# A gated linear attention kernel: one tile per column block of w_in, and the second group's alpha ahead of the first scores

## The chip, the cores and the metric

The kernel runs on one core of a Trainium2 chip. The metric is the device time of one execution in microseconds (us); the time before is the median of three runs. The engines are named as the profile names them: PE is the matrix engine (PEld its weight loads), DVE the vector engine, ACT the scalar engine, POOL the general one, SP the engine that issues most transfers. A name with a q at its end (SPq) is an engine's sequencer.

## The reference

Two blocks follow each other. The first is a gated linear attention with 4 batches, 8 heads, 768 steps and 48 values per head; the second projects its output with `w_in`, runs a decaying sum over time, gates it and projects it with `w_out`. Both weights come as float64.

```python
for t in range(S):                                   # attention, per batch and head
    state = alpha[t, :, None] * state + outer(k[t], v[t])
    y[t] = q[t] @ state
x = y.transpose(0, 2, 1, 3).reshape(B, S, H * D)     # 4 x 768 x 384
proj = x @ w_in                                      # w_in 384 x 1024, float64
val, gate = proj[..., :512], proj[..., 512:]
for t in range(S):
    h = exp(A_log)[0] * h + val[:, t, :]
    ys[:, t, :] = h
out = (gate * sigmoid(gate) * ys) @ w_out            # w_out 512 x 384, float64
```

## The kernel before, in words

The 4 x 768 steps are cut into 12 groups of 256 steps, two chunks (c = 0, 1) of 128 steps each. All instructions stand in an order that is written out by hand, engine by engine in program order; an engine that waits holds up everything behind it on that engine. The steps of one group m:

- Loading: SP issues the transfers of alpha, k, q (`load_natural` for groups 0 to 2, `load_raw` later) and v. The weights follow group 1 on SP's queue: for each of four column blocks i of 128 columns of the value half and of the gate half, `load_w_in(i)` issues eight transfers into `bits_in`, 32 in all; then two transfers bring `w_out` into `bits_out`, and group 2's inputs come behind those.
- `natural_alpha(m)`: PE turns alpha by 8 transposes, ACT copies it into `aT`. `check_alpha(m)`: one ACT instruction (with a read of its sum) that looks whether alpha stays at or below one.
- `products(m)`, a generator: DVE forms the running product `prod` over the group (a scan, L606), then its inverse `inv` (a scan, L618).
- `natural_qk(m, name)`: PE turns k or q, DVE multiplies with `inv` or `prod` into `Z` (L580). In the kernel before, these PSUM tiles come from the pool of the scores' banks.
- `scores(m, c)`: 16 matmuls of k against q into `sc0` and `sc1`. `masks(m, c)`: the triangular mask, on DVE for `sc0` (L660), on ACT (a copy, L658) and POOL (L659) for `sc1`. `keys(m, c)`: PE turns k back, ACT copies it to `ktm` (L643). `state`, `values`, `carried`: matmuls for the running state and the output y. `join(m)`: ACT copies y into `xT`, and six small transfers move its fourth quarter into place (L707); for groups 0 and 1 POOL issues them.
- `project(n, cc)`: six accumulating products of xT with block cc of `w_in`, the value half (pv) and the gate half (pg). `gated(n, cc)`: a DVE scan over pv (hh, L730), ACT's Silu of pg (sg, L735), POOL's product f (L736). `output(n)`: 16 matmuls with `w_out` (the first 12 need the first three blocks of f, the last four the fourth block).

The weights must be made float32 once. `convert(i)` does so for block i of `w_in` (i = 0 to 3) or for a half of `w_out` (i = 4, 5): ACT makes a low part `wr` (L517), DVE forms the high part with a TENSOR_SCALAR (L518) and a SCALAR_TENSOR_TENSOR (L520), and POOL adds the two (L522). The call gives back the addition, so that it can be placed apart: `convert(0)()` or `sums = convert(3)` and later `sums()`. The same instruction order has, before the loop, group 0's and group 1's attention, with the six conversions and `project(0, 0)` to `project(0, 3)` between and behind them; then `output(0)`; then the loop over n = 1 to 11, which mixes the projection of group n with the attention of group n + 1.

`w_in` and `bits_in` are one tile each; a conversion reads a quarter of `bits_in` and writes a quarter of `w_in`, each quarter in strips. The waits between engines and on transfers are set by the program from the tiles that instructions read and write.

`check_w(i)` scans the raw weights' size on DVE (two reductions each), in the loop from n = 3 on. `warm(count)` issues matmuls that nothing reads.

Of the kernel before, what the change touches and what calls it, by code (L numbers as in the profile page):

```python
# [346 lines left out]
def fast(  # L347
# [86 lines left out]

    w_in = const.tile([C, NK, 2, DI], FP32, name="w_in")
    w_out = const.tile([C, NI, DM], FP32, name="w_out")
    NW = NK + 2
    bits_in = const.tile([C, NK, 2 * DI, 2], U32, name="bits_in")
    bits_out = const.tile([C, NI, DM, 2], U32, name="bits_out")

    def load_w_in(i, engine):

        for first_row, size in ((0, D), (D, R)):
            for vg in range(2):
                for s in range(2):
                    row, step = (4 * s * D, D) if size == D else ((4 * s + 3) * D, R)
                    cols = ds(2 * (vg * DI + i * C), 2 * C)
                    engine.dma_start(  # L448
                        out=bits_in[ds(64 * s + first_row, size), :, ds(vg * DI + i * C, C)]
                        .rearrange("p kk n two -> p kk (n two)"),  # L450
                        in_=moe_w_in.bitcast(U32)[ds(row, NK * step), cols]
                        .rearrange("(kk p) n -> p kk n", p=step)[0:size])
# [51 lines left out]
    def convert(i):  # L504


        if i < NI:
            bits = bits_in.rearrange("p kk (vg n) two -> p kk vg n two", vg=2)[:, :, :, ds(i * C, C)]
            w = w_in[:, :, :, ds(i * C, C)]
        else:  # L510
            rows = ds(2 * (i - NI), 2)
            bits, w = bits_out[:, rows, None], w_out[:, rows, None, :]
# [11 lines left out]
    def check_w(i):  # L524
        if i < NK:
            hi = bits_in[:, i, :, 1].bitcast(FP32)
        else:
            hi = bits_out[:, ds(2 * (i - NK), 2)].rearrange("p cc n two -> p (cc n) two")[:, :, 1].bitcast(FP32)
        for t, op in ((wmax, ALU.max), (wmin, ALU.min)):
# [35 lines left out]

    def natural_qk(m, name):

# [3 lines left out]
        for c in range(G):  # L571
            tp = ps_sc.tile([C, 4, C], FP32, tag=f"sc{c}", name="tn")
            for p in range(4):
# [140 lines left out]
    def project(n, cc):  # L714
# [6 lines left out]
        for vg, pj in enumerate((pv, pg)):  # L721
            for kk in range(NK):
                nc.tensor.matmul(pj, w_in[:, kk, vg, ds(cc * C, C)], xT[:, kk, :],  # L723
                                 start=(kk == 0), stop=(kk == NK - 1))
# [73 lines left out]
    for _ in products(0):  # L798
        pass
    for c in range(G):  # L800
        k_times(c)
        q_times(c)
    for c in range(G):
        scores(0, c)
# [3 lines left out]
    for c in range(G):  # L808
        keys(0, c)
    natural_alpha(1)  # L810
    check_alpha(1)
    steps = products(1)
    next(steps)
    next(steps)
    values(0, 0)
# [4 lines left out]
    join(0, (nc.gpsimd, nc.gpsimd))()  # L820
    k_times, q_times = natural_qk(1, "k"), natural_qk(1, "q")
    warm(4)
    for _ in steps:
        pass
    for c in range(G):
        k_times(c)
        q_times(c)
    convert(0)()

# [4 lines left out]
    for c in range(G):  # L834
        keys(1, c)
    convert(1)()
    pj = project(0, 0)
    gated(0, 0, *pj)
    state(1, 0)
# [4 lines left out]
    carried(1, 1)  # L844
    convert(2)()
    join(1, (nc.gpsimd, nc.gpsimd))()
    sums = convert(3)
    pj = project(0, 1)
    gated(0, 1, *pj)
    sums()  # L850
    sums = convert(NI)
    pj = project(0, 2)
    gated(0, 2, *pj)
    sums()
    natural_alpha(2)
    sums = convert(NI + 1)
    pj = project(0, 3)
    gated(0, 3, *pj)
    sums()
    check_alpha(2)  # L860
# [103 lines left out]
```

## Time and profile before

| what | value |
|---|---|
| median of three runs | 327.07 us (324.81 to 328.57) |
| profiled execution | 329.01 us |
| its span, first to last instruction | 327.3 us |
| PE busy | 296.7 us (91%) |
| DVE, ACT, POOL busy | 230.7, 96.9, 115.1 us |
| mean granted clock of PE | 0.961 of full |
| transfers | 39.71 MB, mean 121 GB/s |

A row of the timeline gives the start in the span, the time, the engine, the line of the code, the operation, what is written and read, and how many instructions are merged; in brackets the idle time of that engine before it and what ended it. The granted clock is 1.00 where PE runs at its full level (2.4 GHz) and 0.50 at the lower one (1.2 GHz).

### The profile page before, as it was taken

The numbers are of one execution on the slowest core, as the hardware profiler recorded it, in microseconds if no ns is written. First come the engines' busy times: TensorE is split into PE (matmuls) and PEld (weight loads), VectorE is DVE, ScalarE is ACT, GpSimd is POOL, SyncE is SP. The second block draws the span as 40 slices with busy tenths as digits, with TensorE's granted clock in tenths as the row PEclk, the third lists the DMA queues.
The fourth block names the chain that finished last, engine by engine and source line by source line (L and its number), as shares of the span: only waits on it lengthen the run. The fifth ranks groups of instructions, "written<-read, shape, count | busy, mean of one in ns | idle before, by whom it ended". The sixth has DMA issues, their size and how long they took to land.

```text
span 327.3 us, 6026 instructions
## 1 busy us (share of the span) xinstructions
PE 296.7 (91%) x2355; PEld 232.4 (71%) x2355; DVE 230.7 (70%) x244; ACT 96.9 (30%) x201; POOL 115.1 (35%) x109
## 2 busy tenths in 40 slices
PE   8898089579996999999999999999999999999991
PEld 4485078348865887878868878878688688786870
DVE  3864297958972696898997998989979689432110
ACT  3270226304120433324224224242253143221201
POOL 6032096821800521721704306408133054140120
PEclk9999669959996999999999999999999999999999
DMA  9998899708159904936909819759169220100101
GB/s 135 163 182 194 234 215 218 122 0 203 33 117 214 196 8 119 216 60 170 204 16 246 130 58 225 112 141 215 35 177 199 62 50 11 52 1 14 48 5 55
DMA packets 69165, 39.71 MB, mean 121 GB/s; under 512 B 47492, under 2 KB 68616, under 8 KB 69128
## 3 DMA queue, kind: packets, MB, share of 16 engines
q1 hardware_dynamic: 66736, 38.35, 59.2%
q10 hardware_dynamic: 2008, 0.69, 1.0%
q8 instruction: 20, 0.33, 0.5%
q0 software_dynamic: 384, 0.20, 0.3%
q14 instruction: 17, 0.14, 0.1%
HBM read 33.33 MB, written 4.72 MB: 116 GB/s over the span
## 4 chain that ended last, share of the span: by engine, by line
PE 80%; SPq 7%; DMA 4%; DVE 3%; POOL 2%; issue 1%; ACT 0%; POOLq 0%
PE pv L723 21%; PE o L744 20%; PE pg L723 18%; PE sc L652 6%; PE y L671 6%; DMA bits_in<-in_moe_w_in_dram 4%; SPq L421 4%; PE y L682 3%; PE st L692 3%; SPq L448 2%; PE tp L642 2%; DVE w_out L520 2%; SPq L430 1%; POOL w_out L522 1%; DVE hh L730 1%
## 5 line engine op out<-in xcount | busy, mean ns | idle before, releaser
L736 POOL TENSOR_TENSOR f<-sg,hh 128x256 f32<-128x256 f32 x48 | 60.3, 1257 | 151.8 <-ACT sg L735 135.0
L723 PE MATMUL pv<-xT,w_in 128*128 128x256 f32 x288 | 75.3, 399 | 16.0 <-POOL w_in L522 12.6
L723 PEld LDWEIGHTS pv<-xT,w_in 128*128 128x128 f32 x288 | 54.2, 195 | 29.2 <-POOL w_in L522 13.5
L723 PE MATMUL pg<-xT,w_in 128*128 128x256 f32 x288 | 71.8, 386 | 0.0
L744 PE MATMUL o<-w_out,f 128*128 128x384 f32 x192 | 67.1, 504 | 4.3 <-POOL w_out L522 4.3
L723 PEld LDWEIGHTS pg<-xT,w_in 128*128 128x128 f32 x288 | 56.1, 195 | 8.1
L744 PEld LDWEIGHTS o<-w_out,f 128*128 128x128 f32 x192 | 37.7, 197 | 29.0 <-POOL w_out L522 4.9
L735 ACT ACTIVATE sg<-pg 128x256 f32<-128x256 f32 x48 | 18.4, 383 | 111.6 <-PE pg L723 92.7
L730 DVE TENSOR_TENSOR_SCAN hh<-a_dec,hh,pv 128x256 f32<-128x256 f32 x32 | 23.5, 734 | 38.5 <-PE pv L723 36.6
L659 POOL TENSOR_TENSOR A<-A,mask 128x512 f32<-128x512 f32 x24 | 31.0, 1312 | 28.0 <-ACT A L658 28.0
L606 DVE TENSOR_TENSOR_SCAN prod<-aT,first 128x1024 f32<-128x1024 f32 x12 | 32.9, 2746 | 0.1
L618 DVE TENSOR_TENSOR_SCAN inv<-aT,last 128x1025 f32<-128x1025 f32 x12 | 29.2, 2430 | 0.4
L748 ACT ACTIVATE o_sb<-o 128x384 f32<-128x384 f32 x24 | 11.8, 490 | 54.7 <-PE o L744 54.7
L652 PE MATMUL sc<-Z 48*128 48x128 f32 x384 | 24.8, 278 | 0.0
L652 PEld LDWEIGHTS sc<-Z 48*128 48x128 f32 x384 | 22.5, 188 | 3.2 <-issue 1.7
L671 PE MATMUL y<-A,v 128*64 128x128 f32 x384 | 23.4, 274 | 0.0
L660 DVE TENSOR_TENSOR A<-sc,mask 128x512 f32<-128x512 f32 x24 | 16.5, 691 | 8.0 <-PE sc L652 7.7
L671 PEld LDWEIGHTS y<-A,v 128*64 128x64 f32 x384 | 20.8, 137 | 0.2 <-issue 0.2
L730 DVE TENSOR_TENSOR_SCAN hh<-a_dec,pv 128x256 f32<-128x256 f32 x16 | 10.9, 680 | 11.6 <-PE pv L723 11.6
L597 DVE STREAM_TRANSPOSE aT<-raw_a 128x1024 f32<-128x1024 f32 x9 | 18.3, 2035 | 0.0
L597 DVE STREAM_TRANSPOSE Z<-raw_q 128x1024 f32<-128x1024 f32 x9 | 18.3, 2032 | 0.0
L597 DVE STREAM_TRANSPOSE Z<-raw_k 128x1024 f32<-128x1024 f32 x9 | 18.2, 2022 | 0.0
(87 smaller groups left out, 270.5 us busy)
## 6 DMA issues: line engine op xcount, KB each, us to landing
raw_k<-in_k_dram SPq DMA_DIRECT2D x24, 192.0 KB, 5.1
raw_q<-in_q_dram SPq DMA_DIRECT2D x24, 192.0 KB, 5.6
v<-in_v_dram SPq DMA_DIRECT2D x24, 192.0 KB, 5.0
out_dram<-o_sb SPq DMA_DIRECT2D x24, 192.0 KB, 1.9
raw_a<-in_alpha_dram SPq DMA_DIRECT2D x23, 192.0 KB, 3.8
raw_a<-in_alpha_dram SPq DMA_DIRECT2D x18, 176.0 KB, 4.0
raw_k<-in_k_dram SPq DMA_DIRECT2D x18, 176.0 KB, 5.1
raw_q<-in_q_dram SPq DMA_DIRECT2D x18, 176.0 KB, 4.2
```

What stands on the lines that cost most here:

```text
L597: nc.vector.transpose(out=to.rearrange("p h (c j) -> p h j c", j=NT), in_=raw_bufs[m % NR][name].rearrange("p h (j d) -> p h j d", d=D)[:, ...
L606: nc.vector.tensor_tensor_scan(out=prod, data0=aT[:, 0:4 * GC], data1=first.rearrange("p h n -> p (h n)"), initial=0.0, op0=ALU.mult, op1= ...
L618: nc.vector.tensor_tensor_scan(out=inv[:, ::-1], data0=aT[:, ::-1], data1=last.rearrange("p h n -> p (h n)")[:, 0:4 * GC + 1][:, ::-1], in ...
L652: nc.tensor.matmul(sc[i][:, p, :], Z[rows, p, 1, cols], Z[rows, p, 0, cols], start=True, stop=True)
L659: nc.gpsimd.tensor_mul(A[:, 1], A[:, 1], mb)
L660: nc.vector.tensor_mul(A[:, 0], sc[0], mb)
L671: nc.tensor.matmul(ys[m][i][ds(64 * s, 64), e, ds(c * C, C)], v_sb[:, c, 2 * p + i, :], A[:, i, p, :], start=(c == 0 and e == 0), stop=Fal ...
L723: nc.tensor.matmul(pj, w_in[:, kk, vg, ds(cc * C, C)], xT[:, kk, :], start=(kk == 0), stop=(kk == NK - 1))
L730: nc.vector.tensor_tensor_scan(out=hh, data0=a_dec[:, cc:cc + 1].to_broadcast([C, GC]), data1=pv, initial=prev_h[cc][:, GC - 1:GC] if g el ...
L735: nc.scalar.activation(sg, pg, AF.Silu)
L736: nc.gpsimd.tensor_mul(fs[n][:, cc, :], sg, hh)
L744: nc.tensor.matmul(os[c], fs[n][:, cc, ds(c * C, C)], w_out[:, cc, :], start=(cc == 0), stop=(cc == NI - 1))
```

## The change

`w_in` and `bits_in` become four tiles each, one per column block; the conversion, the projection and the weight check take their block's tile. The weight check goes over six pieces (four blocks, two halves of `w_out`) in place of five. Before the loop the order is written anew: the second group's alpha is turned, checked and its first scan done ahead of the first group's scores; the second group's q goes through the banks `ps_mm`, and its two k products stand ahead of its two q products; two of four warm matmuls go; no conversion stands ahead of the second group's masks; the conversions follow them, each block's ahead of its projection.

```diff
-    w_in = const.tile([C, NK, 2, DI], FP32, name="w_in")
+    w_in = [const.tile([C, NK, 2, C], FP32, name=f"w_in{i}") for i in range(NI)]
-    NW = NK + 2
-    bits_in = const.tile([C, NK, 2 * DI, 2], U32, name="bits_in")
+    NW = NI + 2
+    bits_in = [const.tile([C, NK, 2, C, 2], U32, name=f"bits_in{i}") for i in range(NI)]
...
-                        out=bits_in[ds(64 * s + first_row, size), :, ds(vg * DI + i * C, C)]
+                        out=bits_in[i][ds(64 * s + first_row, size), :, vg]
...
-            bits = bits_in.rearrange("p kk (vg n) two -> p kk vg n two", vg=2)[:, :, :, ds(i * C, C)]
-            w = w_in[:, :, :, ds(i * C, C)]
+            bits, w = bits_in[i], w_in[i]
...
-    def natural_qk(m, name):
+    def natural_qk(m, name, banks=None):
...
-            tp = ps_sc.tile([C, 4, C], FP32, tag=f"sc{c}", name="tn")
+            tp = (banks or ps_sc).tile([C, 4, C], FP32, tag="mm" if banks else f"sc{c}", name="tn")
...
-                nc.tensor.matmul(pj, w_in[:, kk, vg, ds(cc * C, C)], xT[:, kk, :],
+                nc.tensor.matmul(pj, w_in[cc][:, kk, vg, :], xT[:, kk, :],
...
     for _ in products(0):
         pass
+    natural_alpha(1)
+    check_alpha(1)
+    steps = products(1)
     for c in range(G):
         k_times(c)
         q_times(c)
+    next(steps)
+    next(steps)
     for c in range(G):
         scores(0, c)
     nc.scalar.activation(ok[:, 0:1], minus, AF.Silu)
...
     for c in range(G):
         keys(0, c)
-    natural_alpha(1)
-    check_alpha(1)
-    steps = products(1)
-    next(steps)
-    next(steps)
     values(0, 0)
...
-    k_times, q_times = natural_qk(1, "k"), natural_qk(1, "q")
-    warm(4)
+    k_times, q_times = natural_qk(1, "k"), natural_qk(1, "q", ps_mm)
+    warm(2)
     for _ in steps:
         pass
-    for c in range(G):
-        k_times(c)
-        q_times(c)
-    convert(0)()
+    for times in (k_times, q_times):
+        for c in range(G):
+            times(c)
...
-    convert(1)()
-    pj = project(0, 0)
-    gated(0, 0, *pj)
+    convert(0)()
     state(1, 0)
...
-    convert(2)()
-    join(1, (nc.gpsimd, nc.gpsimd))()
-    sums = convert(3)
-    pj = project(0, 1)
-    gated(0, 1, *pj)
-    sums()
...
+    moves = join(1, (nc.gpsimd, nc.gpsimd))
+    convert(1)()
+    moves()
+    for cc in range(NI):
+        pj = project(0, cc)
+        gated(0, cc, *pj)
+        convert(cc + 2)()
     natural_alpha(2)
```

The order on DVE, in the kernel before, from the last multiplication of the second group's q (Z is the pair of turned k and q) to the first scan over a projection (hh):

```order
L580 TENSOR_TENSOR Z<-tn,prod 128x4x128
L518 TENSOR_SCALAR w_in<-bits_in 128x6x128
L520 SCALAR_TENSOR_TENSOR w_in<-bits_in,w_in 128x6x128
L660 TENSOR_TENSOR A<-sc_407,mask 128x512
L660 TENSOR_TENSOR A<-sc_418,mask 128x512
L518 TENSOR_SCALAR w_in<-bits_in 128x6x128
L520 SCALAR_TENSOR_TENSOR w_in<-bits_in,w_in 128x6x128
L730 SCALAR_TENSOR_TENSOR hh<-a_dec,pv 128x256
```

The same stretch of DVE now:

```order
L580 TENSOR_TENSOR Z<-tn,prod 128x4x128 x2
L660 TENSOR_TENSOR A<-sc_406,mask 128x512
L660 TENSOR_TENSOR A<-sc_417,mask 128x512
L518 TENSOR_SCALAR w_in_89<-bits_in_94 128x768
L520 SCALAR_TENSOR_TENSOR w_in_89<-bits_in_94,w_in_89 128x768
L518 TENSOR_SCALAR w_in_90<-bits_in_95 128x768
L520 SCALAR_TENSOR_TENSOR w_in_90<-bits_in_95,w_in_90 128x768
L730 SCALAR_TENSOR_TENSOR hh<-a_dec,pv 128x256
```

The first conversion, which reads a transferred weight, now stands behind the second group's masks, and each conversion reads and writes a tile of its own.

The order on ACT, in the kernel before, around the first group's mask copies (A<-sc), behind the check of its alpha (junk); the table load and the write to ok prepare the Silu:

```order
L591 ACTIVATE junk,above<-raw_a_81,minus 128x768
L805 ACT_TABLE_LOAD
L805 ACTIVATE ok<-minus 128x1
L658 ACTIVATE A<-sc_257 128x512
L658 ACTIVATE A<-sc_268 128x512
L643 ACTIVATE ktm_100<-tp 128x512
L643 ACTIVATE ktm_101<-tp 128x512
L564 ACTIVATE aT<-tn 128x4x128 x2
L591 ACTIVATE junk,above<-raw_a_84,minus 128x768
```

The same stretch of ACT now:

```order
L591 ACTIVATE junk,above<-raw_a_81,minus 128x768
L564 ACTIVATE aT<-tn 128x4x128 x2
L591 ACTIVATE junk,above<-raw_a_84,minus 128x768
L810 ACT_TABLE_LOAD
L810 ACTIVATE ok<-minus 128x1
L658 ACTIVATE A<-sc_280 128x512
L658 ACTIVATE A<-sc_291 128x512
L643 ACTIVATE ktm_106<-tp 128x512
L643 ACTIVATE ktm_107<-tp 128x512
```

The second group's alpha (copies and check) moved ahead of the table load and of the first group's mask copies.

The order on POOL, in the kernel before, from the first addition of a conversion to the last:

```order
L522 TENSOR_TENSOR w_in<-w_in,wr 128x6x128
L659 TENSOR_TENSOR A<-A,mask 128x512 x2
L522 TENSOR_TENSOR w_in<-w_in,wr 128x6x128
L736 TENSOR_TENSOR f<-sg,hh 128x256
L522 TENSOR_TENSOR w_in<-w_in,wr 128x6x128
L707 DMA xT<-xT 16x256 x6
L736 TENSOR_TENSOR f<-sg,hh 128x256
L522 TENSOR_TENSOR w_in<-w_in,wr 128x6x128
L736 TENSOR_TENSOR f<-sg,hh 128x256
L522 TENSOR_TENSOR w_out<-w_out,wr 128x768
L736 TENSOR_TENSOR f<-sg,hh 128x256
L522 TENSOR_TENSOR w_out<-w_out,wr 128x768
```

The same stretch of POOL now, from the second group's masks on:

```order
L659 TENSOR_TENSOR A<-A,mask 128x512 x2
L522 TENSOR_TENSOR w_in_89<-w_in_89,wr 128x768
L522 TENSOR_TENSOR w_in_90<-w_in_90,wr 128x768
L707 DMA xT<-xT 16x256 x6
L736 TENSOR_TENSOR f<-sg,hh 128x256
L522 TENSOR_TENSOR w_in_91<-w_in_91,wr 128x768
L736 TENSOR_TENSOR f<-sg,hh 128x256
L522 TENSOR_TENSOR w_in_92<-w_in_92,wr 128x768
L736 TENSOR_TENSOR f<-sg,hh 128x256
L522 TENSOR_TENSOR w_out<-w_out,wr 128x768
L736 TENSOR_TENSOR f<-sg,hh 128x256
L522 TENSOR_TENSOR w_out<-w_out,wr 128x768
```

The masks moved ahead of the first addition, and the second addition and the six transfers ahead of the first f; from there additions and f alternate.

## Rows read from the trace of the kernel before

**Rows 1.** Stretches: busy us of PE, PEld, DVE, ACT, POOL; PE's granted clock; DMA.

```profile
67.30:74.16 6.86, 6.86 (x12) 3.71 (x13) 2.48 (x2) 0.44 (x1) 0.00 (x0) 0.57 0.00 0
...
97.80:101.22 3.42, 0.01 (x1) 0.04 (x1) 0.00 (x0) 0.49 (x1) 0.00 (x0) 0.89 1.05 145
101.22:327.30 226.08, 218.65 (x1758) 175.41 (x1758) 162.54 (x168) 66.09 (x142) 73.49 (x58) 0.98 0.50 108
```

**Rows 2.** Timeline of PE, from the first scores to the second output.

```profile
14.96 2.14 PE L652 MATMUL sc<-Z 48*128 48x128 f32 x32
...
24.60 3.60 PE L782 MATMUL warm<-ident 128*128 128x512 f32 x8
28.13 2.06 PE L652 MATMUL sc<-Z 48*128 48x128 f32 x32
...
42.15 2.93 PE L723 MATMUL pv<-xT,w_in 128*128 128x256 f32 x6 [10.94 <-POOL w_in L522]
...
53.42 1.56 PE L723 MATMUL pv<-xT,w_in 128*128 128x256 f32 x6
...
56.11 1.04 PE L563 MATMUL tn<-ident,raw_a 128*128 128x128 f32 x8
...
67.30 7.03 PE L744 MATMUL o<-w_out,f 128*128 128x384 f32 x12 [4.32 <-POOL w_out L522]
74.16 1.04 PE L574 MATMUL tn<-ident,raw_k 128*128 128x128 f32 x8
...
92.47 5.32 PE L744 MATMUL o<-w_out,f 128*128 128x384 f32 x16
```

**Rows 3.** Timeline of DVE, the same stretch.

```profile
16.22 1.52 DVE L660 TENSOR_TENSOR A<-sc,mask 128x512 f32<-128x512 f32 x2 [0.69 <-PE sc L652]
...
20.30 2.29 DVE L606 TENSOR_TENSOR_SCAN prod<-aT,first 128x1024 f32<-128x1024 f32 x1
...
23.05 2.29 DVE L618 TENSOR_TENSOR_SCAN inv<-aT,last 128x1025 f32<-128x1025 f32 x1
...
38.58 0.56 DVE L518 TENSOR_SCALAR w_in<-bits_in 128x768 uint32<-128x768 uint32 x1 [10.65 <-DMA bits_in<-in_moe_w_in_dram]
39.17 0.96 DVE L520 SCALAR_TENSOR_TENSOR w_in<-bits_in,w_in 128x768 uint32<-128x768 uint32 x1
...
56.20 5.83 DVE L520 SCALAR_TENSOR_TENSOR w_out<-bits_out,w_out 128x768 uint32<-128x768 uint32 x1
...
62.86 2.79 DVE L606 TENSOR_TENSOR_SCAN prod<-aT,first 128x1024 f32<-128x1024 f32 x1
```

**Rows 4.** Timeline of ACT up to the second group's alpha.

```profile
8.67 1.28 ACT L805 ACT_TABLE_LOAD   x1
...
16.25 0.60 ACT L658 ACTIVATE A<-sc 128x512 f32<-128x512 f32 x1 [6.08 <-PE sc L652]
...
18.70 1.23 ACT L564 ACTIVATE aT<-tn 128x512 f32<-128x512 f32 x2
19.83 0.93 ACT L591 ACTIVATE junk<-raw_a,minus 128x768 bf16<-128x768 f32 x1
```

**Rows 5.** Timeline of POOL, from the first masks to the last conversion.

```profile
17.00 2.51 POOL L659 TENSOR_TENSOR A<-A,mask 128x512 f32<-128x512 f32 x2 [11.05 <-ACT A L658]
...
51.54 1.82 POOL L522 TENSOR_TENSOR w_in<-w_in,wr 128x768 int32<-128x768 int32 x1 [3.19 <-ACT wr L517]
53.31 2.96 POOL L707 DMA_DIRECT2D xT<-xT  x6
...
58.73 0.72 POOL L736 TENSOR_TENSOR f<-sg,hh 128x256 f32<-128x256 f32 x1
...
63.46 3.78 POOL L522 TENSOR_TENSOR w_out<-w_out,wr 128x768 int32<-128x768 int32 x1
```

**Rows 6.** The eight transfers of block 0 of w_in: issue time in ns, first and last start; landing.

```profile
L448 SPq DMA_DIRECT2D bits_in<-in_moe_w_in_dram x8: 422/435/1512, 18.0 to 23.1; - x8
...
DMA to landing us min/median/max: 3.7/5.2/5.5
```

More of the change, by code (lines that the diff above doesn't have):

```diff
@@ L524, in check_w @@
     def check_w(i):
-        if i < NK:
-            hi = bits_in[:, i, :, 1].bitcast(FP32)
+        if i < NI:
+            hi = bits_in[i].rearrange("p kk vg n two -> p (kk vg n) two")[:, :, 1].bitcast(FP32)
         else:
-            hi = bits_out[:, ds(2 * (i - NK), 2)].rearrange("p cc n two -> p (cc n) two")[:, :, 1].bitcast(FP32)
+            hi = bits_out[:, ds(2 * (i - NI), 2)].rearrange("p cc n two -> p (cc n) two")[:, :, 1].bitcast(FP32)
         for t, op in ((wmax, ALU.max), (wmin, ALU.min)):
@@ L844, in fast @@
     carried(1, 1)
-    convert(2)()
-    join(1, (nc.gpsimd, nc.gpsimd))()
-    sums = convert(3)
-    pj = project(0, 1)
-    gated(0, 1, *pj)
-    sums()
[L851 to L854, printed above, removed]
+    moves = join(1, (nc.gpsimd, nc.gpsimd))
[5 more added lines that the diff above has]
+        convert(cc + 2)()
     natural_alpha(2)
[L856 to L859, printed above, removed]
     check_alpha(2)
```

## The prediction

> **What bounds the kernel now.** I read the busy time by stretches first, then PE's timeline, then for each long idle time of PE the timelines of the engines that ended it. From 101.22 us to the end PE is busy 218.65 of 226.08 us [rows 1]: that part goes as fast as PE's work, which the change leaves alone, so only the time at which PE gets there can move. Ahead of it the reader is to see three idle times of PE: 10.94 us before 42.15, 4.32 us before 67.30 [rows 2], and 3.42 us from 97.80 [rows 1]. The first two end with an addition of `convert` on POOL. Behind the first stands a transfer: DVE had waited 10.65 us at the first conversion, until 38.58, for `bits_in` [rows 3], with the second group's masks queued behind that wait on DVE and on ACT. Yet block 0's eight transfers were all issued by 23.1, and none took over 5.5 us to land [rows 6], so they were there by 28.6. The conversion waited for all 32 because they write one tile. The second idle time is the end of a chain of six conversions that this wait started late: first multiplication at 38.58, last addition at 63.46 + 3.78 = 67.24 [rows 3, 5]. Both idle times left PE at a low granted clock: the value half of a projection took 2.93 us at 42.15 against 1.56 at 53.42, and the last 12 matmuls of the first output took 7.03 us at a mean granted clock of 0.57, where 16 took 5.32 later [rows 1, 2].
>
> **The change part by part.** I follow one quantity, the start of the third group's k transposes, 74.16 now [rows 2]; everything behind it should shift with it.
>
> *Alpha of group 1 ahead of the first scores.* PE does 8 transposes (1.04, by the same form at 56.11) before the scores, which now start at 14.96 [rows 2]: 16.0. ACT copies alpha once half the transposes are through, about 15.6 (taken between 14.96 and 16.0). From those copies to the end of check and read it needed 18.70 to about 20.85 (19.83 + 0.93 and a short read), 2.15; then the table load 1.28 and its small follower about 0.2 [rows 4]. The table load had lain in idle time at 8.67; now it stands in the way. So ACT's first mask copy starts at 15.6 + 2.15 + 1.5 = 19.25 in place of 16.25, 3.0 later, and POOL's masks, which follow by 0.75 and take 2.51, end at 22.5 in place of 19.51 [rows 4, 5]. From there to the second group's scores it was 28.13 - 19.51 = 8.62. That contained the 8 transposes (1.04), now gone, and four warm matmuls of 3.60, now two (-1.8) [rows 2]: 22.5 + 8.62 - 1.04 - 1.8 = 28.3. By DVE: its first scan starts some 3.1 earlier (20.30 less 3.1), takes in the two masks (1.52) on the way and perhaps waits for POOL's masks (0 to 2.51), so `inv`, which ended at 25.34, ends between 23.8 and 26.3 [rows 3]; the four multiplications, 0.6 each, and the scores follow, 27 to 28.5. The second group's scores thus start where they did, 28.3 against 28.13. This part gains nothing by itself: 3 us lost on ACT, 2.8 us of PE's work saved. The bounds are -1 and +1 us, inside those below. The new banks for q and the order k, k, q, q are nothing: all four products must be there before both chunks' scores, and the three mm banks are free then.
>
> *Masks of group 1 ahead of the conversions, and a tile per block.* With scores at 28.3, POOL's masks start 2.04 later (17.00 against 14.96), 30.35, and end at 32.9; DVE's start 1.26 later and end at 31.1 [rows 2, 3, 5]. Block 0 has landed (28.6 at the latest), so TENSOR_SCALAR 0.56 and SCALAR_TENSOR_TENSOR 0.96 follow at once. Between both ends the price is open, because DVE and POOL do not run freely beside each other: a SCALAR_TENSOR_TENSOR of 0.96 took 5.83 under POOL's work at 56.20, and an addition took 3.78 where DVE's scan of 2.79 ran, against 1.82 [rows 3, 5]. Freely: the addition begins at 32.9 and ends at 34.8. Wholly one after the other: 30.35 + 2.51 + 1.55 + 0.2 + 1.82 = 36.4. I take 36.0, near the second, since these rows show it. Then `project(0, 0)` starts at 36.0 in place of 42.15. Its other inputs are there: the second group's matmuls end some 2 us after POOL's masks, about 35. The other blocks need nothing of the queue: the last of all 32 transfers landed at 38.58, when block 3 is converted after 41.
>
> *The chain of conversions.* From 36.0 POOL has five additions (1.82), four f (0.72) and the six transfers (2.96) [rows 5]: 14.9 us. Four of the additions need a SCALAR_TENSOR_TENSOR that DVE can do only between POOL's operations: 4 x (0.96 + 0.15) = 4.4. The one for block 2 runs under the six transfers. So the last addition ends at 36.0 + 14.9 + 4.4 = 55.3, in place of 67.24. PE's part is shorter: a project takes 56.11 - 53.42 = 2.69 [rows 2], and each f waits for its project, which is why I let no f run ahead. What falls out against now: the masks inside the chain (2.51), the addition that stood 3.19 us for ACT's part, which was behind state copies, and the scan between [rows 3, 5]. Open bounds: DVE's next scan slips in ahead of the last addition, +2.8; the SCALAR_TENSOR_TENSORs hide, but then PE sets the pace, -2.5.
>
> The Trainium skill (SBUF, "Who interferes with whom") says that a DVE instruction with two SBUF inputs and a POOL instruction that reads SBUF exclude each other, and that whichever starts first keeps the ports for the whole instruction. By that rule a waiting SCALAR_TENSOR_TENSOR loses one POOL operation at most, and the 4.4 us stand. The row at 56.20 differs: 4.87 us is more than any two of POOL's operations there, so DVE can be passed by several. By the row the fifth, too, would stand directly ahead of its addition, and the chain would end at 56.4.
>
> *Output and third group.* From the last addition PE needed 74.16 - 67.24 = 6.9 us at the low clock. At the full one, 12 matmuls take 12/16 of 5.32 = 4.0, that is 3.0 less [rows 2]: 3.9. So the transposes start at 55.3 + 3.9 = 59.2, 15.0 us earlier. DVE's third-group scans follow the last conversion (55.3 + 2 x 2.29 + 0.4 = 60.3, four multiplications to 62.7); PE reaches the scores that need them at 59.2 + 1.75 (16 transposes) + 2.69 + 0.6 = 64.2, so they stay covered, by 1.5 us. SP's transfers for groups 2 and 3 are in the queue already and set by bandwidth; the 3.42 us at 97.80, in the shifted place, stay: they end with transfers that follow the third group's `join`, whose order is the same.
>
> *The weight check* gets two reductions more on DVE, each over less. DVE is busy 162.54 of 226.08 us there [rows 1]; even at 2.8 us each they fit its idle time. Without that cover they would cost 5.6.
>
> Sum: 15.0 us. The profiled execution took 329.01, 1.94 over the median, so 314.0 on its scale and **312.1** as a median.
>
> **The rivals.** *Low clock between the conversions (20%).* PE would idle from 41.6 to 44.4 for block 2's addition and some 2.3 us before the output's last 12 matmuls. The shortest idle time that was followed by a low clock is 3.42 [rows 1]; mine are shorter but close. Price: a project at half rate +2.7, the output +3.0; both leave 9.3, 317.8. The Trainium skill (TensorE: Matmul & The Clock Gate, "HAM oscillation — how this bites in real kernels") has this as its rule: idle gaps in PE's stream bring the half rate back. The trace agrees for 10.94, 4.32 and 3.42 us.
>
> *The split does not free the wait (5%).* If the first conversion still waited until 38.58, the masks would no longer stand behind it; its addition would end where it did (42.1) and the chain, 19.3, at 61.4: 5.9 earlier, with 3.0 more if the clock is full. Median 318 to 321. Against: each block's transfers have a tile of their own.
>
> *More than I see (6%):* the idle time at 97.80 ends without the low clock (the next project ran at half rate there), or bounds fall together: 18 to 19 us, 308.
>
> *An unforeseen wait takes part of it (10%)*, gain 3 to 9.
>
> *Slower (4%): the low clock stays.* From 34.8 on PE's stream is thin (2.7 us of work for each 4 to 5 us), and with the low clock each us of full-speed work costs one us more. It decides from 15 us of full-speed work at half rate; if both that stretch (some 18 us of PE work) and the first loop round were run so, the end would come 3 to 10 us later, 330 to 337. Against: after 42.15 and 67.30 PE was back at full rate within one or two matmul groups.
>
> **How the numbers follow.** The forecast (55%) has its own range of 12 to 18.7 us gained, 308.4 to 315. To hold 8 in 10 I add the low clock (317.8) and half of the split case: **308 to 319**. A change of under 1% is what a measurement here cannot tell from none. Faster by over 1%: 0.55 + 0.20 + 0.05 + 0.06 and half or more of the 0.10: 0.91. Within 1%: 0.04. Slower: 0.05.
>
> **What would show it.** Right: no idle time of DVE that ends with `bits_in`; `project(0, 0)` near 36; the last addition near 55; the third group's k transposes near 59; the rest unchanged but shifted. Wrong: scores of the second group after 30 (ACT's table load costs more), a last addition after 58 (DVE and POOL in each other's way), a granted clock near 0.5 between 41 and 60, or an idle time of PE in the loop longer than 3.42.

## The result, and the profile after

| what | before | after |
|---|---|---|
| median | 326.82 us (324.81 to 328.57, 4 executions) | 311.97 us (310.09 to 314.21, 4 executions) |
| profiled execution | 329.01 us | 310.16 us |
| its span | 327.3 us | 308.4 us |
| mean granted clock of PE | 0.961 | 0.997 |

The ratio is 0.955 [0.945, 0.9651]; the forecast was 312.1 us. The four executions of after stand in two pairs: 310.09 and 310.16 us at a mean granted clock of 0.997, 313.77 and 314.21 at 0.982 and 0.985. The profiled one is of the first pair. In the runs below, an execution more than 1.5% above the fastest of its kernel is left out of the median; this happened once, at 315.83 us, with alpha moved back.

Three stretches of after, which answer to [rows 1] (columns as there):

```profile
55.69:59.66 3.97, 3.97 (x13) 2.33 (x13) 3.87 (x4) 0.45 (x1) 0.00 (x0) 1.00 1.09 249
83.30:86.31 3.01, 0.00 (x1) 0.03 (x1) 0.00 (x0) 0.49 (x1) 0.00 (x0) 1.00 1.10 176
86.31:308.40 222.09, 215.66 (x1758) 173.25 (x1758) 162.76 (x170) 66.23 (x142) 73.34 (x58) 1.00 0.50 110
```

The idle time in the loop now ends at 86.31, where it ended at 101.22: 14.91 us of the gain lie ahead of it. Behind it the kernel is 3.99 us shorter (222.09 against 226.08) although its work is the same: before, the clock was low there for some 7 us (0.51 from 100.40 to 107.30), and in this execution of after it is not. The first product behind that idle time, in the kernel before:

```profile
101.22 2.90 PE L723 MATMUL pv<-xT,w_in 128*128 128x256 f32 x6 [3.42 <-issue]
```

The timeline of PE in after, which answers to [rows 2]; its last line is the same product:

```profile
27.77 2.06 PE L652 MATMUL sc<-Z 48*128 48x128 f32 x32
...
35.58 1.56 PE L723 MATMUL pv<-xT,w_in 128*128 128x256 f32 x6 [0.52 <-POOL w_in L522]
...
44.37 1.56 PE L723 MATMUL pv<-xT,w_in 128*128 128x256 f32 x6 [2.56 <-POOL w_in L522]
...
55.69 4.14 PE L744 MATMUL o<-w_out,f 128*128 128x384 f32 x12 [2.21 <-POOL w_out L522]
59.66 1.04 PE L574 MATMUL tn<-ident,raw_k 128*128 128x128 f32 x8
...
86.31 1.53 PE L723 MATMUL pv<-xT,w_in 128*128 128x256 f32 x6 [3.02 <-issue]
```

The idle time of 10.94 us is 0.52, that of 4.32 is 2.21, and a new one of 2.56 stands ahead of `project(0, 2)`. DVE, against [rows 3], goes from its last mask straight into the first conversion, with no wait for `bits_in`:

```profile
29.92 0.69 DVE L660 TENSOR_TENSOR A<-sc,mask 128x512 f32<-128x512 f32 x1 [0.20 <-PE sc L652]
30.53 0.89 DVE L518 TENSOR_SCALAR w_in<-bits_in 128x768 uint32<-128x768 uint32 x1
31.45 1.93 DVE L520 SCALAR_TENSOR_TENSOR w_in<-bits_in,w_in 128x768 uint32<-128x768 uint32 x1
...
41.35 3.39 DVE L518 TENSOR_SCALAR w_in<-bits_in 128x768 uint32<-128x768 uint32 x1
44.77 1.37 DVE L520 SCALAR_TENSOR_TENSOR w_in<-bits_in,w_in 128x768 uint32<-128x768 uint32 x1
```

ACT's table load now lies on the way to the first masks, against [rows 4]:

```profile
17.73 1.28 ACT L810 ACT_TABLE_LOAD   x1
19.02 0.20 ACT L810 ACTIVATE ok<-minus 128x1 f32<-128x1 f32 x1
19.13 1.07 ACT L658 ACTIVATE A<-sc 128x512 f32<-128x512 f32 x2
```

POOL, against [rows 5]; the brackets are what its additions waited for:

```profile
33.52 2.00 POOL L522 TENSOR_TENSOR w_in<-w_in,wr 128x768 int32<-128x768 int32 x1 [0.96 <-DVE w_in L520]
37.09 1.81 POOL L522 TENSOR_TENSOR w_in<-w_in,wr 128x768 int32<-128x768 int32 x1 [1.56 <-ACT wr L517]
38.83 2.97 POOL L707 DMA_DIRECT2D xT<-xT  x6
...
44.27 1.06 POOL L736 TENSOR_TENSOR f<-sg,hh 128x256 f32<-128x256 f32 x1
46.28 1.81 POOL L522 TENSOR_TENSOR w_in<-w_in,wr 128x768 int32<-128x768 int32 x1 [0.96 <-DVE w_in L520]
...
53.83 1.80 POOL L522 TENSOR_TENSOR w_out<-w_out,wr 128x768 int32<-128x768 int32 x1 [0.96 <-DVE first L603]
```

The last bracket names a small instruction of DVE; what the addition needs there is the SCALAR_TENSOR_TENSOR of 52.32 just ahead of it, as in the two brackets before it.

### The profile page after: what moved, and what is told of

Its sections match the earlier page's. It is cut to its first block, busy times and chain, and to the rows that moved or that the text cites. A ratio compares the mean times of both kernels' runs of the same rounds, so it can differ in the third digit from the quotient of the medians.

```text
span 308.4 us, 6047 instructions
## 1 busy us (share of the span) xinstructions
PE 288.0 (93%) x2351; PEld 226.9 (74%) x2351; DVE 233.0 (76%) x246; ACT 97.2 (32%) x201; POOL 113.4 (37%) x109
## 4 chain that ended last, share of the span: by engine, by line
PE 78%; SPq 8%; DMA 5%; DVE 5%; issue 1%; POOL 1%; ACT 0%
PE pv L723 20%; PE o L744 20%; PE pg L723 18%; PE sc L652 6%; PE y L671 6%; SPq L421 4%; DMA bits_in<-in_moe_w_in_dram 3%; PE y L682 3%; PE st L692 3%; SPq L449 3%; PE tp L642 2%; DMA bits_out<-in_moe_w_out_dram 1%; SPq L430 1%; DVE w_out L518 1%; DVE w_in L518 1%
## 5 line engine op out<-in xcount | busy, mean ns | idle before, releaser
L736 POOL TENSOR_TENSOR f<-sg,hh 128x256 f32<-128x256 f32 x48 | 61.1, 1272 | 144.2 <-ACT sg L735 142.3
L723 PE MATMUL pv<-xT,w_in 128*128 128x256 f32 x288 | 72.6, 388 | 7.5 <-POOL w_in L522 4.5
L723 PE MATMUL pg<-xT,w_in 128*128 128x256 f32 x288 | 70.0, 379 | 0.0
L723 PEld LDWEIGHTS pv<-xT,w_in 128*128 128x128 f32 x288 | 52.6, 190 | 20.7 <-POOL w_in L522 6.0
L744 PE MATMUL o<-w_out,f 128*128 128x384 f32 x192 | 64.4, 488 | 2.2 <-POOL w_out L522 2.2
L723 PEld LDWEIGHTS pg<-xT,w_in 128*128 128x128 f32 x288 | 54.7, 190 | 7.4
L744 PEld LDWEIGHTS o<-w_out,f 128*128 128x128 f32 x192 | 36.2, 190 | 25.6 <-POOL w_out L522 3.1
L735 ACT ACTIVATE sg<-pg 128x256 f32<-128x256 f32 x48 | 18.5, 385 | 109.2 <-PE pg L723 96.3
L659 POOL TENSOR_TENSOR A<-A,mask 128x512 f32<-128x512 f32 x24 | 30.3, 1284 | 31.5 <-ACT A L658 31.5
L606 DVE TENSOR_TENSOR_SCAN prod<-aT,first 128x1024 f32<-128x1024 f32 x12 | 34.0, 2837 | 0.1
L618 DVE TENSOR_TENSOR_SCAN inv<-aT,last 128x1025 f32<-128x1025 f32 x12 | 30.0, 2497 | 0.4
```

The lines of the kernel that those rows point to most:

```text
L606: nc.vector.tensor_tensor_scan(out=prod, data0=aT[:, 0:4 * GC], data1=first.rearrange("p h n -> p (h n)"), initial=0.0, op0=ALU.mult, op1= ...
L618: nc.vector.tensor_tensor_scan(out=inv[:, ::-1], data0=aT[:, ::-1], data1=last.rearrange("p h n -> p (h n)")[:, 0:4 * GC + 1][:, ::-1], in ...
L659: nc.gpsimd.tensor_mul(A[:, 1], A[:, 1], mb)
L723: nc.tensor.matmul(pj, w_in[cc][:, kk, vg, :], xT[:, kk, :], start=(kk == 0), stop=(kk == NK - 1))
L735: nc.scalar.activation(sg, pg, AF.Silu)
L736: nc.gpsimd.tensor_mul(fs[n][:, cc, :], sg, hh)
```

## Experiments: the parts of the change

The theory is the prediction's: a conversion waited for all 32 transfers because they wrote one tile; with a tile per block the chain of conversions starts earlier and everything behind it shifts. The rivals: the new order does it, or the granted clock does.

**Only the tiles.** The kernel before, with the tile lines of the diff and its own order.

```diff
-    w_in = const.tile([C, NK, 2, DI], FP32, name="w_in")
+    w_in = [const.tile([C, NK, 2, C], FP32, name=f"w_in{i}") for i in range(NI)]
...
-    bits_in = const.tile([C, NK, 2 * DI, 2], U32, name="bits_in")
+    bits_in = [const.tile([C, NK, 2, C, 2], U32, name=f"bits_in{i}") for i in range(NI)]
```

> The kernel before with the tiles per column block alone; its order stays. My theory (the change gains because the chain of conversions on DVE and POOL no longer starts at 38.58 behind the last of 32 transfers): the first conversion starts near 28, right behind the second group's Z, the first projection near 32 to 33 (xT of group 0 has landed at 31.4), the last addition of a conversion near 57 to 58 in place of 67.2, and PE has no long idle time near 31 to 42, so its clock stays: 10 to 13 us less than before. Rival A (the new order of the attention, alpha ahead above all, gives the gain): at most 2 us less. Rival C (the clock gives it): as much as the idle times of PE vanish, 5 to 8 us less.

Measured: 314.53 us (312.68 to 315.84), ratio 0.958 [0.9524, 0.9635].

**Only the order.** The kernel after with those lines taken back:

> The changed kernel with w_in and bits_in as one tile each again; its new order stays. My theory: the first conversion waits until about 38.6 again, but the second group's masks no longer stand behind it; first projection near 42, last addition near 61: 6 to 9 us less than before, 6 to 9 more than the changed kernel. Rival A (the order gives the gain): as fast as the changed kernel within 2 us. Rival C (the clock): PE idles from 35 to 42, the clock falls: 2 to 6 us less than before.

Measured: 321.35 us (319.52 to 323.65), ratio 0.9755 [0.9686, 0.9825]. Two rows of DVE and PE in the kernel with the order alone, then three of POOL and PE in the kernel with the tiles alone:

```profile
38.99 0.56 DVE L519 TENSOR_SCALAR w_in<-bits_in 128x768 uint32<-128x768 uint32 x1 [8.33 <-DMA bits_in<-in_moe_w_in_dram]
...
63.74 5.83 PE L745 MATMUL o<-w_out,f 128*128 128x384 f32 x12 [2.21 <-POOL w_out L523]
```

```profile
29.60 1.82 POOL L521 TENSOR_TENSOR w_in<-w_in,wr 128x768 int32<-128x768 int32 x1 [2.55 <-DVE w_in L519]
...
51.83 3.78 POOL L521 TENSOR_TENSOR w_out<-w_out,wr 128x768 int32<-128x768 int32 x1
...
55.66 5.83 PE L743 MATMUL o<-w_out,f 128*128 128x384 f32 x12 [4.35 <-POOL w_out L521]
```

With one tile the first conversion waits until 38.99, as before (38.58), whatever the order. With a tile per block the chain ends at 55.6 even in the old order, 11.6 before the old 67.24 and where after ends it. So the tiles alone give 14.5 us (329.05, the median of before beside these runs, less 314.53), more than the 10 to 13 expected, since the last addition came at 55.6 and not at 57 to 58. With the order alone it came at 63.7, later than the 61 expected, and the gain is 7.7. The two gains do not add (14.5 and 7.7, together 14.9): they shorten the same chain. What the order adds to the tiles is an idle time of 2.21 in place of 4.35 ahead of the first output; whether it gains time is not shown, since the two ratios' intervals overlap (0.9524 to 0.9635, and 0.945 to 0.9651 for after). Nor does a run split `w_in` and `bits_in` one by one; the wait that went away ended with `bits_in`.

**Alpha back behind the keys.** The kernel after, with one part of the new order undone:

```diff
-    natural_alpha(1)
-    check_alpha(1)
-    steps = products(1)
...
     for c in range(G):
         keys(0, c)
+    natural_alpha(1)
+    check_alpha(1)
+    steps = products(1)
+    next(steps)
+    next(steps)
     values(0, 0)
```

> The changed kernel with the second group's alpha (turn, check, first scan) back behind the first group's keys. My theory: this part gains nothing, the second group's scores stay within 1 us of 28 and the time within 1 us of the changed kernel. Rival A: the time goes back by 5 us or more towards before. Rival B (alpha ahead costs on ACT what it saves on PE, net a loss): 1 to 2 us less than the changed kernel.

Measured: 311.46 us (311.1 to 314.13), ratio 0.9465 [0.9399, 0.9531]; the second group's scores at 28.1 (after: 27.77), the last addition ends at 55.9 (55.63). This part gains nothing, as predicted.

## Experiments: the clock

**The kernel before with its idle times filled.**

```diff
     convert(1)()
+    warm(12)
     pj = project(0, 0)
...
+    warm(5)
     output(0)
...
         output(n)
+        if n == 1:
+            warm(4)
```

> The kernel before with matmuls that nothing reads in PE's three idle times (12 ahead of the first projection, 5 ahead of the first output, 4 behind the second output). It measures the clock alone: the chain of conversions stays where it was. My theory: the last addition stays near 67 and only half-rate work is made good, 2 to 3 us at each output-side stall, together 4 to 7 us less than before, the first idle time giving next to nothing because POOL sets the pace behind it. Rival C (most of the gain is the clock's): 10 us or more less than before.

Measured: 322.47 us (322.24 to 323.14), ratio 0.9806 [0.9752, 0.9859]. Two stretches of it:

```profile
0.00:101.00 101.00, 93.33 (x649) 64.18 (x650) 70.20 (x77) 30.93 (x59) 42.89 (x51) 1.00 0.89 159
101.00:320.00 219.00, 213.57 (x1750) 171.39 (x1748) 162.13 (x168) 66.18 (x142) 73.55 (x58) 1.00 0.49 108
```

The clock was full throughout and the last addition ended at 68.1. So low clock cost the kernel before 329.05 - 322.47 = 6.6 us (4.6 to 8.2 by the ratio's interval), and the chain the rest: 68.1 - 55.6 = 12.5, by which this kernel is longer than after at full clock (322.5 - 310.1 = 12.4). The two parts make 19.0 us, as the two profiled executions do (329.01 - 310.16 = 18.9). The medians are only 14.9 apart, since two of after's four executions still had a low clock somewhere.

**The kernel after with its idle times filled.**

```diff
         convert(cc + 2)()
+        if cc == 1:
+            warm(2)
...
+    warm(2)
     output(0)
...
         output(n)
+        if n == 1:
+            warm(3)
```

> The changed kernel with matmuls that nothing reads in its three longest idle times of PE (2 ahead of the third block's projection, 2 ahead of the first output, 3 behind the second output). Its executions lay in two clumps, near 310.1 and near 313.9. Theory (the low clock that some executions have behind these idle times makes the upper clump): granted clock full in all of it, all times within 1 us of 310, median some 2 us under the changed kernel's. Rival (the clumps come from transfers or from the chip): both clumps stay, median within 1 us of 312.

Measured: 310.94 us (310.76 to 311.15), ratio 0.9484 [0.9441, 0.9526]. The additions end where they did (55.7). The four times lie within 0.4 us, where those of after lie 4.1 apart: with the mean clocks of after's executions (0.982 and 0.985 in the slower pair) this says that the slower pair got a low clock behind some of the three idle times. The chip is not the cause: on the same one, the kernel with the transfers on ACT and its idle times unfilled (below) went from 310.9 to 313.67. No execution of the slower pair was profiled, but one like it was, in the kernel with alpha moved back (314.13 us, mean clock 0.985, last addition at 55.9). It had the low clock at two places, where after has 4.14 and 1.53:

```profile
55.95 5.83 PE L744 MATMUL o<-w_out,f 128*128 128x384 f32 x12 [2.21 <-POOL w_out L522]
...
88.38 2.90 PE L723 MATMUL pv<-xT,w_in 128*128 128x256 f32 x6 [3.13 <-issue]
```

Its span is 312.3 us against after's 308.4, about the distance of the two pairs. With the idle times filled the median fell by 1.0, half of what was expected, because after's median lies between its pairs and the added matmuls cost a little (310.94 against 310.1).

## Experiments: the chain on POOL

**The conversions' first halves one block further ahead**, so that no SCALAR_TENSOR_TENSOR stands directly ahead of its addition:

```diff
+    sums = {2: convert(2)}
     for cc in range(NI):
         pj = project(0, cc)
+        if cc + 3 < NI + 2:
+            sums[cc + 3] = convert(cc + 3)
         gated(0, cc, *pj)
-        convert(cc + 2)()
+        sums[cc + 2]()
```

> The changed kernel with the ACT and DVE parts of conversions 2 to 5 one block further ahead; POOL's order and all work stay. My term: three additions stand 0.96 us each for a SCALAR_TENSOR_TENSOR that DVE could do only between POOL's operations, and f is slowed by a TENSOR_SCALAR (1.05 against 0.74), 3.9 us in all. Theory A (it is the order: done ahead, these parts fall into POOL's idle time near 36 and under the six transfers): the last addition ends near 52 in place of 55.6, 3 to 4 us less. Rival B (the two engines exclude each other, so every DVE part costs POOL its time wherever it stands): the last addition stays within 1 us of 55, no gain.

Measured: 315.48 us (313.3 to 317.17), ratio 0.9615 [0.9547, 0.9684], 3.5 over after. Neither answer came. Of DVE and of POOL in this kernel:

```profile
43.95 2.04 DVE L518 TENSOR_SCALAR w_out<-bits_out 128x768 uint32<-128x768 uint32 x1 [1.01 <-DMA bits_out<-in_moe_w_out_dram]
```

```profile
47.73 0.89 POOL L736 TENSOR_TENSOR f<-sg,hh 128x256 f32<-128x256 f32 x1 [2.15 <-DVE hh L730]
...
56.25 0.73 POOL L736 TENSOR_TENSOR f<-sg,hh 128x256 f32<-128x256 f32 x1 [2.71 <-ACT sg L735]
```

The conversions now came to weights that had not landed, and with DVE and ACT waiting for those, hh and sg were queued behind, for which POOL waited. The last addition ended at 58.7. The edit moved a wait for transfers into the chain and so says nothing on the lock between DVE and POOL.

**Without the SCALAR_TENSOR_TENSOR**, in the kernel with filled idle times:

```diff
-        nc.vector.scalar_tensor_tensor(out=t, in0=hi, scalar=0xC0000000, in1=t,
-                                       op0=ALU.bitwise_and, op1=ALU.bitwise_or)
```

> Kernel after with its three idle times filled, and with the SCALAR_TENSOR_TENSOR of each conversion left out, so the weights lack their upper two bits (sign among them). The prediction's term: four of them stand between POOL's additions at 0.96 + 0.15, 4.4 us. Theory: without them POOL's work follows without waits, 14.9 us from project(0, 0), and f is back near 0.72: last addition at 50.5 to 51.5, the median 4 us under the filled kernel's. Rival: the TENSOR_SCALAR ahead of it takes the same place between the additions; then only 4 x 0.4 us are gained, last addition at 54, under 2 us.

Measured: 308.22 us (307.71 to 308.88), ratio 0.9421 [0.9367, 0.9475], 2.7 under the filled kernel by the medians, though the two ratios' intervals overlap. Of POOL and DVE:

```profile
37.02 1.81 POOL L520 TENSOR_TENSOR w_in<-w_in,wr 128x768 int32<-128x768 int32 x1 [2.74 <-ACT wr L517]
...
44.20 1.05 POOL L734 TENSOR_TENSOR f<-sg,hh 128x256 f32<-128x256 f32 x1
...
47.71 0.73 POOL L734 TENSOR_TENSOR f<-sg,hh 128x256 f32<-128x256 f32 x1 [0.69 <-ACT sg L733]
...
51.31 1.82 POOL L520 TENSOR_TENSOR w_out<-w_out,wr 128x768 int32<-128x768 int32 x1
```

```profile
37.14 2.11 DVE L518 TENSOR_SCALAR w_in<-bits_in 128x768 uint32<-128x768 uint32 x1
...
41.09 3.58 DVE L518 TENSOR_SCALAR w_in<-bits_in 128x768 uint32<-128x768 uint32 x1
```

Between the two answers: the last addition ends at 53.1. From the second addition's start to the last one's end it takes 16.1 us, against 18.5 in after, so the SCALAR_TENSOR_TENSORs there were worth 2.4 net. Three of them stand directly ahead of an addition in that stretch, 3 x 1.11 = 3.3 in the prediction's sum. Without them POOL waited 0.9 us for sg, which follows PE's projections: PE began to set the pace, the bound that the prediction had put at 2.5. The TENSOR_SCALAR, which I had counted as free, waits beside POOL as well (3.58 against 0.56 in [rows 3]), and the f at its end still took 1.05.

**The second group's six xT transfers issued by ACT**, behind the conversion of cc = 1, so that they leave POOL's chain:

```diff
-    moves = join(1, (nc.gpsimd, nc.gpsimd))
+    moves = join(1, (ACT, ACT))
     convert(1)()
-    moves()
...
         convert(cc + 2)()
+        if cc == 1:
+            moves()
```

> The changed kernel with the second group's six small transfers issued by ACT behind the second block's conversion, not by POOL between two additions. Theory: POOL's chain loses 2.97 us, the third block's projection starts near 42.3 in place of 44.4 and the last addition ends 2 to 3 us earlier: 2 to 3 us less. Rival: ACT's issues (some 0.6 each) delay its parts of the conversions, and the last addition stays within 1 us: no gain.

Measured: 312.06 us (310.9 to 313.67), ratio 0.9504 [0.9456, 0.9552]. The last addition came 1.6 earlier, at 54.0, and yet the third group's k transposes at 59.68 as in after. The stretch of the first output's last 12 matmuls says why, with PE's clock at 0.59 where after had 1.00 in the same place:

```profile
54.00:58.10 4.10, 4.09 (x8) 2.29 (x9) 4.00 (x4) 0.00 (x0) 0.00 (x0) 0.59 1.10 232
```

The same edit with filled idle times:

> Kernel after with matmuls that nothing reads in its three idle times of PE (two ahead of project(0, 2), two ahead of output(0), three behind output(1)), and the second group's six xT transfers issued by ACT behind the conversion of cc = 1 in place of POOL. Theory (the clock hid the gain of the transfers moved alone): the last addition ends at 54.0 as it did with the transfers moved alone, the first output starts there at the full clock, the third group's k transposes come 3.97 later, at 58.0, and the loop's first round 1.6 earlier than in the filled kernel: 309.3 as a median. Rival (the loop's first round is set by transfers, whatever PE does ahead): project(2, 0) stays at 86.3 to 86.7, 310.9.

Measured: 309.24 us (308.72 to 309.67), ratio 0.9447 [0.9406, 0.9488]; the last addition ends at 53.9, the k transposes start at 57.9, `project(2, 0)` at 84.9. The theory's numbers hold: what is taken from the chain arrives at the end when the clock does not take it back.

## Experiments: the idle time in the loop

The prediction let the 3.42 us ahead of `project(2, 0)` stay, "they end with transfers". **The third group's six xT transfers on POOL:**

```diff
-            join(m, (SP, ACT))()
+            join(m, (nc.gpsimd, nc.gpsimd) if m == 2 else (SP, ACT))()
```

> The changed kernel with the third group's six small transfers issued by POOL, not half by SP behind nine other transfers. PE waits 3.02 us for them at 86.3. Theory (SP's queue is what is late): the projection starts near 84, the idle time is 0 to 1.5 us, and without it the clock does not fall: 2 to 4 us less in the median. Rival (the landing, 4 to 5 us after a POOL issue, is as late): no change.

Measured: 313.53 us (312.54 to 314.74), ratio 0.9563 [0.9511, 0.9615]. `project(2, 0)` started at 83.3 without idle time, but 3.39 us of it came back ahead of `project(3, 0)`, with a clock of 0.53 behind it (109.10 to 112.70), and the median did not fall. So three groups were moved (`m in (2, 3, 4)`), in the kernel with filled idle times and the second group's transfers on ACT:

> The same, without the three matmuls behind output(1), and with the six xT transfers of the third, fourth and fifth group issued by POOL in place of SP and ACT. Theory (the idle time ahead of project(2, 0) is the wait for xT transfers that stand behind input transfers on SP's queue): no idle time of over 1 us behind output(1), output(2) and output(3), project(2, 0) at 81.5 to 82; 3.0 + 1.6 less than the filled kernel, 306.5 to 307. Rival (the inputs are short of time and the loop must wait for them once, wherever that is): an idle time of 3 us or more comes back within the next rounds, 309 to 311.

Measured: 311.16 us (310.55 to 312.04), ratio 0.9509 [0.9467, 0.9551]. The rival's time: three rounds ran without idle time, and then

```profile
151.17 2.90 PE L723 MATMUL pv<-xT,w_in 128*128 128x256 f32 x6 [3.11 <-issue]
```

This is the first group whose transfers SP and ACT issue again. SP's own waits tell why, here around that place:

```profile
SPq L406 <- DMA xT<-xT: 10.8, 2, 10.5
```

and in after from 60 to 90, with its timeline of SP (idle from 68.49 to 78.42):

```profile
SPq L406 <- DMA xT<-xT: 10.1, 2, 9.8
```

```profile
65.03 3.46 SPq L406 DMA_DIRECT2D raw_k<-in_k_dram  x4
78.42 1.86 SPq L406 DMA_DIRECT2D raw_q<-in_q_dram  x4
80.32 1.29 SPq L430 DMA_DIRECT2D v<-in_v_dram  x2
81.92 2.61 SPq L707 DMA_DIRECT2D xT<-xT  x3
```

Meanwhile the transfers were not short of bandwidth; the last two columns of this stretch of after are the DMA share and GB/s:

```profile
72.00:78.00 6.00, 6.00 (x93) 5.33 (x94) 5.71 (x7) 1.80 (x4) 2.77 (x2) 1.00 0.01 3
```

A load of q waits 9.8 us for an xT transfer that has nothing to do with it. The program's listing shows the link, for after: transfers of SP and of ACT share eight counters, and each waits for the one that had its counter last.

```
ACT 55 L707 DMA xT_810<-xT_810 16x256 [waits DMAHW4_49,Activation_49]
SP  78 L406 DMA raw_q0_82<-in_q_dram 32x4x384 [waits DMAHW4_49,DVE_49,PE_49]
SP  84 L707 DMA xT_810<-xT_810 16x256 [waits ... DMAHW2_49 ...]
```

ACT's xT transfers cannot go before attention has made xT; the load of q waits behind them on the counter; SP's half of the same xT stands behind that load; and PE waits for it. The times agree: ACT issued its three from 76.56, they took 1.8 us to land (median), and SP's load of q began at 78.42.

The counters also say why later rounds do not wait. They are given out in turn, and in the listing of after the loads of this one round are the only inputs in the loop that follow an xT transfer of ACT on a counter. In the kernel with the third group's transfers on POOL it is the loads of the next round, and in the one with three groups' on POOL those of the sixth group's: the rounds with the idle time in each (86.31, 109.07, 151.17).

**All xT transfers of the loop on POOL**, that is those of the third group and of all behind it; the second group's, ahead of the loop, stay on ACT:

> The kernel with the joins of three groups on POOL, now with the six xT transfers of every group issued by POOL. Theory (the idle time belongs to the first join whose transfers SP issues behind input transfers, and is paid once by whichever group that is): with no such join it never comes, project(2, 0) at 81.4 and rounds of 21.7 to 22.6 to the end; 3.5 under the kernel with filled idle times and the transfers of the second group on ACT (309.24), so 305.7 as a median. Rival (the loop must wait once for its inputs, or POOL's 2.96 us in each round hold up its f): an idle time of 2 us or more further on, or longer rounds, 308 to 312.

Measured: 305.85 us (305.29 to 306.29), ratio 0.934 [0.9298, 0.9381], the best version here, 6 us under after. The time is the theory's. Its wording is too wide, since SP issues xT behind input transfers in every round of after and only one round pays; the counters tell them apart. PE at the place, and SP's queue ahead of it:

```profile
82.11 1.53 PE L723 MATMUL pv<-xT,w_in 128*128 128x256 f32 x6 [0.33 <-DMA xT<-xT]
```

```profile
68.83 1.80 SPq L406 DMA_DIRECT2D raw_k<-in_k_dram  x4
70.73 2.56 SPq L406 DMA_DIRECT2D raw_q<-in_q_dram  x4
```

The loads of q go right behind those of k, and no idle time of 1 us is left in the loop. POOL's six issues per round (2.94 us) fit its idle time.

## Why the prediction was right

| step | predicted | measured |
|---|---|---|
| scores of the second group | 28.3 | 27.77 |
| `project(0, 0)` | 36.0 (34.8 to 36.4) | 35.58 |
| last addition ends | 55.3 | 55.63 |
| third group's k transposes | 59.2 | 59.66 |
| idle time in the loop, moved | stays 3.42 | 3.02 |
| median | 312.1 | 311.97 |

*The wait for 32 transfers* was the cause, as read from [rows 3, 6]: with the tiles it is gone, and with the tiles undone it is back (8.33 us).

*The chain* came out at 20.05 us from `project(0, 0)` to the last addition, against 14.9 + 4.4 = 19.3, but its terms were off both ways. The waits for SCALAR_TENSOR_TENSORs were three of 0.96, 2.9 in place of 4.4. The fourth, of block 1, ended at 33.88 + 2.46 = 36.34 and is hidden by a term that was not in the sum: the second addition waited 1.56 us, until 37.09, for ACT's part, which stood behind the copies of `join(1)`; without the SCALAR_TENSOR_TENSORs it began at 37.02 all the same. And f took 0.74 and three times about 1.05, 3.9 in place of 2.9, since the lock between DVE and POOL, which I had put on the SCALAR_TENSOR_TENSOR alone, slows f beside the TENSOR_SCALAR too. That these errors cancel to 0.8 us is luck.

The Trainium skill (SBUF, "Who interferes with whom") names tensor_scalar among the operations that can, in their two-port modes, take the port pair that VectorE shares with GpSimd. The runs agree that it is held up beside POOL's work (3.39 in after, 3.58 without the SCALAR_TENSOR_TENSOR). The page also says that whoever issues first gets the pair for the whole instruction; by that the TENSOR_SCALAR of 41.35, which began ahead of f (41.82) and of the addition behind it, should have gone first. It ended at 44.74, after both: the trace differs. POOL's issue of the transfers, which went on until 41.80, does not explain it: in the kernel with the tiles alone a TENSOR_SCALAR inside those six issues (at 42.53) took 0.53.

*The masks, alpha and the table load* were right: ACT's first mask copy at 19.13 against 19.25, and alpha ahead gains nothing in a run of its own.

*The clock* was the step with the wrong shape. I let it be either the forecast (full between the conversions, low behind the loop's idle time as before), or a rival at 317.8 (20%), or "more than I see" at 308 (6%). It varies from execution to execution: at full clock throughout, after takes 310.1, which is near that last rival; with a low clock somewhere it takes 314. The median is close to 312.1 because it lies between two pairs, and that is luck: the sum gave the profiled execution 314.0 and it took 310.16, as the 15.0 us ahead of the loop came as forecast (14.5 at the k transposes) and the 3.99 us of clock behind the loop's idle time came on top. Idle times of 2.2 us ahead of the first output were followed by a clock of 1.00 (after) and of 0.59 (the transfers on ACT), and the one of 3.02 by 1.00, where 3.13 was followed by the low one (alpha moved back), so the shortest idle time in [rows 1] was no limit either way.

The Trainium skill (TensorE: Matmul & The Clock Gate, "HAM oscillation — how this bites in real kernels") has idle gaps in PE's stream as the cause; the runs agree where filling them with matmuls took the low clock away, in the kernel before (6.6 us) and in after. Why one idle time, 2.21 us ahead of the same matmuls, was followed by either level stays open.

*The idle time in the loop* stayed, as predicted, but the reason given, transfers "set by bandwidth", was wrong. The DMA share was 0.01 while SP's load of q waited (72 to 78 in after); [rows 1] had a hint, 0.00 from 67.30 to 74.16, when SP's queue stood still behind the first output. It was a wait between queues that shared counters set; with the loop's xT transfers off these counters it is 0.33. The round in which it falls fits the listings of three kernels; no run changed the counters alone.

## What to carry to other kernels

Where an engine waits for a transfer, compare the landing times of the data it reads with the end of its wait: if they differ by much, it may wait for a neighbour in the same tile, and a tile per consumer tests that (here it was the cure). When two changes shorten one chain, do not add their gains, and fill what idle times are left before judging the second, or the clock hides it. When an idle time moves on by one round after its transfers were moved, look at the issuing queue's own waits for a transfer that has nothing to do with the waiting one.

## What the runs showed of the hardware

- A TENSOR_SCALAR with one SBUF input of 128x768 took 0.56 us alone and 3.39 to 3.58 beside POOL's f and additions; a waiting operation of DVE was passed by two POOL operations (after, 41.35) and by four (before, 56.20, a SCALAR_TENSOR_TENSOR of 5.83 against 0.96).
- At the same places, idle times of 2.21 and 3.02 us (after) were followed by a clock of 1.00, and of 2.20 (the transfers on ACT) or 2.21 and 3.13 (alpha moved back) by the low one; the executions of one program stood in pairs 4 us apart. A few matmuls in those places brought four executions to within 0.4 us.
- Six small transfers issued by POOL took 2.94 us of its time, but off the counters of SP's and ACT's queues no load waited for them: 309.24 to 305.85, 3.4 us.
